# A gated feed-forward kernel: the first weights of block 3 issued later than those of block 2

## The chip, the cores and the metric

The kernel runs on one core of one Trainium2 chip. The metric is the device time of one execution in microseconds (us). A profile covers a slightly shorter span, from the program's first instruction to its last (297.6 us for a run timed at 299.36 us).

## The reference

```python
B, S, D, F = 32, 32, 1024, 3584        # x: (B, S, D), weights scaled by 0.05, all bf16
def reference(x, w_gate, w_up, w_down):
    return (_gelu(x @ w_gate) * (x @ w_up)) @ w_down
```

There are 1024 rows of x. The contraction over D is done in 8 blocks of 128, called block 0 to block 7 below.

## The kernel before

A small program builder records operations in order and derives semaphore waits from what each reads (`r`) and writes (`w`). All operations are emitted from a helper, so most lines of the profile carry the helper's line number (L98). They are told apart by tile names: `wg` and `wu` are the gate and up weights, `xT` the transposed x, `xn` the untransposed first part of x, `ps` the accumulators.

From 0.77 us the matrix engine runs 8 matmuls on constants, called warm-up matmuls below. The real work should start at once, but x must first be transposed and the weights must first arrive. Blocks 0 and 1 of x come as plain loads and are transposed on the matrix engine. Blocks 2 to 7 come by transposing loads on the sync queue. The first group of weights comes in pieces, on the sync and the scalar queue.

```python
NX = 2
for i, eng in enumerate(("sp", "act")):                     # x of blocks 0 and 1, untransposed
    pr.add(eng, "dma_start", xn[...], x_r[...], w=[("xn", i)], dma=f"xn{i}")
for k in range(NX):
    load_w("sp", "g", 0, k, k + 1)                          # gate weights of block k, 128 KB
    load_w("act", "u", 0, k, k + 1)                         # up weights of block k, 128 KB
...
for k0, k1 in ((2, 3), (3, 4), (4, 5), (5, 6), (6, 8)):
    load_x(0, k0, k1)                                       # transposing loads, sync queue
load_w("act", "g", 0, 2, 4)                                 # weights of blocks 2 and 3: 256 KB
load_w("act", "u", 0, 2, 4)                                 #   and another 256 KB
pr.add("act", "activation", warm[:, 0:1], const0, ACTF.Gelu_apprx_tanh)
for k in range(NX):                                         # transpose blocks 0 and 1, copy to xT
    ...
    pr.add("dve", "tensor_copy", xT[:, k, i * 256:(i + 1) * 256], half, r=[("ps", b)],
           w=[("x", k, 0) if i == 0 else ("x", k, "b")])
# ... [cut] then, for the first 512 rows: blocks 0 to 5, each 4 gate and 4 up matmuls;
# after the last matmul of block 0 the scalar queue issues the weights of blocks 4 and 5,
# after the last one of block 1 those of blocks 6 and 7:
if k < 2:
    load_w("act", "g", 0, 2 * k + 4, 2 * k + 6, r=[("mm", k)])
    load_w("act", "u", 0, 2 * k + 4, 2 * k + 6)
```

## Time and profile before

| What | Value |
|---|---|
| time, first 3 runs | 300.06 us median (299.14 to 300.2) |
| span of the profiled run | 297.6 us |
| matrix engine busy | 294.3 us |
| start-to-start time of two matmuls, 512 columns | 0.216 us |
| hole before the matmuls of block 2 | 0.35 us |
| hole after that, to the end | none |

The page of the kernel before starts with the busy time of each engine and the granted clock of the matrix engine (its clock as a share of full speed, in tenths) in 40 slices. It also names the chain of work that ended last.

```profile
span 297.6 us, 2575 instructions
PE 294.3 (99%) x1388; PEld 78.2 (26%) x808; DVE 42.7 (14%) x68; ACT 37.3 (13%) x67; POOL 0.7 (0%) x6
PEclk9999999999999999999999999999999999999999
PE 96%; DMA 2%; SPq 0%; issue 0%; ACT 0%
PE ps L98 54%; PE ps L163 42%; DMA xT<-in_x_dram 2%; SPq L98 0%; ACT xT L98 0%
```

The matrix engine is the bound. Only 2% of the chain is something else: a transposing load of x. The chain in order of time, for the first 12 us (start, duration, what), shows which one:

```profile
2.21 6.22 DMA xT<-in_x_dram
8.43 0.14 issue
8.56 3.61 PE ps L98 x16
```

The load of x block 2 was issued at 2.21 us and landed at 8.43 us. The matmuls of block 2 start at 8.56 us. What that costs is read from the timeline of the matrix engine from 7 to 9.2 us, whose first and last group are cut by that window (start, busy time, group, and in brackets the idle time before it):

```profile
6.70 0.81 PE L98 MATMUL ps<-xT,wg 128*128 128x512 bf16 x3
7.35 1.03 PE L98 MATMUL ps<-xT,wu 128*128 128x512 bf16 x4
8.56 0.81 PE L98 MATMUL ps<-xT,wg 128*128 128x512 bf16 x3 [0.19 <-DMA xT<-in_x_dram]
```

The idle time in brackets counts from the modelled end of the last matmul, and matmuls overlap. So the cost is read from the starts. Four matmuls take 4 x 0.216 = 0.863 us, and block 2 could have started at 7.35 + 0.863 = 8.21 us. It started 0.35 us later. Below, "hole" always means this: a start-to-start time minus 0.216 us.

### The profile page before, as it was taken

How to read it: one execution, taken by the hardware profiler on the slowest of the kernel's cores; microseconds unless marked ns; L12 is line 12 of the kernel's file. 1: busy time of each engine (PE TensorE's matmuls, PEld its weight loads, DVE VectorE, ACT ScalarE, POOL GpSimd, SP SyncE). 2: the span in 40 equal slices, each digit the busy share in tenths (PEclk: the TensorE clock that was granted, in tenths of full speed). 3: DMA queues.
4: the chain of work that ended last, by engine and by line, in shares of the span. 5: the costliest groups of instructions: out<-in, count | busy, mean ns of one | idle time of the engine just before them, and what ended most of it. 6: DMA issues, size and time to landing. Idle time of an engine off the chain costs nothing.

```text
span 297.6 us, 2575 instructions
## 1 busy us (share of the span) xinstructions
PE 294.3 (99%) x1388; PEld 78.2 (26%) x808; DVE 42.7 (14%) x68; ACT 37.3 (13%) x67; POOL 0.7 (0%) x6
## 2 busy tenths in 40 slices
PE   8999999999999999999999999999999999999997
PEld 4444322222222222222222222222222222222244
DVE  1030311111221111111111122110000000000000
ACT  1030411111111111221111111110000000000010
POOL 0000000000000000000000000000000000000000
PEclk9999999999999999999999999999999999999999
DMA  7999743006708409321030040000101101011011
GB/s 207 252 241 353 226 134 134 9 0 189 234 2 270 154 2 330 94 76 65 0 139 4 0 141 0 0 2 0 35 0 35 37 0 35 0 37 35 0 35 35
DMA packets 28842, 26.37 MB, mean 89 GB/s; under 512 B 8352, under 2 KB 25248, under 8 KB 28832
## 3 DMA queue, kind: packets, MB, share of 16 engines
q1 hardware_dynamic: 26640, 24.25, 26.3%
q10 hardware_dynamic: 2192, 1.97, 2.2%
q8 instruction: 8, 0.13, 0.2%
q14 instruction: 2, 0.02, 0.0%
HBM read 22.28 MB, written 2.10 MB: 82 GB/s over the span
## 4 chain that ended last, share of the span: by engine, by line
PE 96%; DMA 2%; SPq 0%; issue 0%; ACT 0%
PE ps L98 54%; PE ps L163 42%; DMA xT<-in_x_dram 2%; SPq L98 0%; ACT xT L98 0%
## 5 line engine op out<-in xcount | busy, mean ns | idle before, releaser
L98 PE MATMUL ps<-xT,wg 128*128 128x512 bf16 x256 | 90.2, 379 | 0.4 <-DVE xT L98 0.2
L98 PE MATMUL ps<-xT,wu 128*128 128x512 bf16 x256 | 90.2, 379 | 0.0
L98 PE MATMUL ps<-wd,hT 128*128 128x512 bf16 (+2 forms) x280 | 86.6, 358 | 0.0
L163 PE MATMUL ps<-wd,hT 128*128 128x512 bf16 x196 | 74.3, 379 | 0.0
L163 PE MATMUL ps<-xT,wg 128*128 128x512 bf16 x192 | 72.8, 379 | 0.0
L163 PE MATMUL ps<-xT,wu 128*128 128x512 bf16 x192 | 72.8, 379 | 0.0
L98 DVE TENSOR_TENSOR hT<-g,ps 128x512 bf16<-128x512 f32 x56 | 36.4, 685 | 158.5 <-PE ps L98 158.5
L98 ACT ACTIVATE g<-ps 128x512 f32<-128x512 f32 x56 | 30.8, 595 | 160.4 <-PE ps L98 160.4
L98 PEld LDWEIGHTS ps<-wd,hT 128*128 128x128 bf16 x280 | 26.0, 98 | 71.3 <-issue 65.8
L98 PEld LDWEIGHTS ps<-xT,wu 128*128 128x128 bf16 x256 | 25.0, 98 | 71.7 <-issue 64.1
L98 PEld LDWEIGHTS ps<-xT,wg 128*128 128x128 bf16 x256 | 24.9, 98 | 72.0 <-issue 64.8
L98 DVE CAST xT<-ps 128x512 bf16<-128x512 f32 (+1 forms) x8 | 5.4, 680 | 89.6 <-ACT xT L98 79.8
L98 ACT ACTIVATE xT<-ps 128x512 bf16<-128x512 f32 (+1 forms) x9 | 5.0, 558 | 94.6 <-PE ps L98 94.6
L98 PE MATMUL ps<-const-bfloat16-1.0 128*128 128x1024 fp8e4 (+1 forms) x8 | 3.0, 558 | 0.8 <-PEq L310 0.8
L98 PEld LDWEIGHTS ps<-const-bfloat16-1.0 128*128 128x256 fp8e4 x8 | 1.7, 218 | 1.9 <-issue 1.9
L98 ACT ACT_TABLE_LOAD x1 | 1.3, 1283 | 3.4 <-issue 3.4
L98 DVE COPY xT<-ps 128x256 bf16<-128x256 bf16 x4 | 0.9, 286 | 4.1 <-PE ps L98 4.1
L98 PE MATMUL ps<-ident,xn 128*128 128x128 bf16 x8 | 0.9, 278 | 0.0
L98 PEld LDWEIGHTS ps<-ident,xn 128*128 128x128 bf16 x8 | 0.6, 124 | 0.2
L98 POOL TENSOR_SCALAR_AFFINE_SELECT ident<-ident 128x128 bf16<-128x128 bf16 x1 | 0.3, 292 | 0.2 <-POOL ident L98 0.2
L98 POOL MEMSET ident<- 128x128 bf16 x1 | 0.2, 204 | 0.3 <-POOLq L310 0.3
L98 ACT ACTIVATE warm<-const-float32-0.0 128x1 f32<-128x1 f32 x1 | 0.2, 202 | 0.0
(4 smaller groups left out, 0.4 us busy)
## 6 DMA issues: line engine op xcount, KB each, us to landing
wd<-in_w_down_dram SPq DMA_DIRECT2D x7, 1024.0 KB, 5.4
wg<-in_w_gate_dram SPq DMA_DIRECT2D x6, 1024.0 KB, 7.4
wu<-in_w_up_dram SPq DMA_DIRECT2D x6, 1024.0 KB, 9.7
out_dram<-xT SPq DMA_DIRECT2D x15, 128.0 KB, 1.7
wg<-in_w_gate_dram ACTq DMA_DIRECT2D x3, 256.0 KB, 4.5
wu<-in_w_up_dram ACTq DMA_DIRECT2D x3, 256.0 KB, 4.9
wg<-in_w_gate_dram SPq DMA_DIRECT2D x2, 128.0 KB, 3.2
wu<-in_w_up_dram ACTq DMA_DIRECT2D x2, 128.0 KB, 3.5
```

Source lines behind the costliest of these rows:

```text
L98: ins = name(eng, *args, **kw) if callable(name) else getattr(eng, name)(*args, **kw)
L163: return eng.add_instruction(mybir.InstMatmult(start_tensor_calc=start, stop_tensor_calc=stop, ldweights=False, name=nc.get_next_instructi ...
```

## The change

The intent is to let x of block 2 land sooner. Its packets share the DMA engines with 512 KB of weights, half of which (block 3) is not needed for another 1.7 us. The change splits those weights and holds back the half for block 3 until the copy of x block 1.

```diff
-        load_w("act", "g", 0, 2, 4)
-        load_w("act", "u", 0, 2, 4)
+        load_w("act", "g", 0, 2, 3)
+        load_w("act", "u", 0, 2, 3)
         pr.add("act", "activation", warm[:, 0:1], const0, ACTF.Gelu_apprx_tanh)
         for k in range(NX):
             ...
+        load_w("act", "g", 0, 3, 4, r=[("x", 1, 0)])
+        load_w("act", "u", 0, 3, 4)
```

## The prediction

> **What bounds the kernel.** The matrix engine. In the profile page it is busy 294.3 of 297.6 us; the chain of waits is 96% matmuls and 2% one DMA, the transposing load of x. In the timeline one matmul starts per 0.216 us (863 ns for four) from 8.56 us to the end, granted clock 1.00. Nothing after 8.56 us waits for data. Ahead of that are two holes: 0.2 us at 4.76 us (the copy of x block 0, untouched by the change) and one at block 2. Four matmuls of block 1 start at 7.35, so block 2 could start at 8.21; it starts at 8.56, just after the transposing load of x block 2 landed at 8.43 (6.2 us after its issue at 2.21; the other transposes of the first half took 4.7 to 5.3, those of the second half, with quieter queues, 3.5 to 3.7). So the whole prize is about 0.35 us, 0.12%.
>
> **What the change does.** Before, the scalar queue issues 256 KB of gate weights (2.27 us, landed 6.72) and 256 KB of up weights (2.75, landed 8.28) for blocks 2 and 3. After, only the halves for block 2 go then; 256 KB for block 3 wait for the third vector copy (copies run 4.07 to 5.01), so until about 4.8 us. Two more DMA issues (about 0.45 us each) run on the scalar queue from 4.8 to 5.8, before its next issue at 6.68, which waits for the matrix engine anyway.
>
> The Trainium skill, "DMA: Bandwidth & Descriptors", sections "Queues, rings and completion order" and "Issuing engines are not separate DMA queues", says both queues share the same 16 engines, taking turns by packet. The trace agrees: in the packet records the 256-byte packets of x block 2 (about 32 an engine, 18 to 24 ns each) spread over 4.6 to 7.0 us while some 33 weight packets of 1 KB an engine (46 to 73 ns) stand in the other queue. With 16 of them gone I estimate 16 x 55 ns = 0.9 us off the load of x block 2: landing at 7.0 to 7.6 instead of 8.43. That removes the wait at block 2, and no more.
>
> **What it may cost.** Block 3 would be needed at 9.94 (gate) and 10.8 (up). Issued at 4.85 and 5.3, and taking 4 to 4.9 us as the other weights of that time, they land near 9.0 and 9.8: slack about 1 us, thin, since they now meet the transposes of blocks 3 and 4. A miss would give back 0.2 to 1 us.
>
> **Predicted.** Most likely the wait vanishes: 300.06 - 0.35 = 299.7 us, less than the run spread of 1.06 us. Range 298.9 to 300.6. Faster by over 2%: 0.01; within 2%: 0.98; slower by over 2%: 0.01.
>
> **What would show it.** Timeline: block 2 starts near 8.2 and no start-to-start step above 0.25 us afterwards; the chain of waits no longer holds the transposing load of x; span near 297.2. DMA issue list: gate and up weights in pieces of 128 KB, block 3 issued near 4.85. The last 280 us are unchanged.
>
> **What would make it wrong.** The landing of x block 2 does not hang on the weights (its completion records came late, amid a stretch of stalled packets at 7.2 to 8.2 us, in which only 157 GB/s moved): then block 2 stays at 8.5. Or the later weights queue behind the transposes' descriptors (the gate weights issued at 6.68 had no packet before 9.0) and block 3 waits: a new hole near 10 us, 0.2 to 1 us slower.

## The result, and the profile after

A ratio here is the mean time of one kernel's fast runs over that of the other's fast runs of the same rounds, so it is not quite the ratio of the medians. Executions over 1.5% slower than the fastest of the same kernel are left out of the means.

The first measurement gave 300.26 us median (6 runs, 299.37 to 1792.36) beside 300.13 us for the kernel before (6 runs). The ratio was 1.0001, with a 95% interval of 0.9976 to 1.0025. No difference.

One run took 1792 us, and the profile happened to fall on it. Nearly every matmul in it was slow while the vector and scalar engines were not. The first lines and three groups of its page (after the bar: busy us, mean ns of one, idle before):

```profile
span 1790.6 us, 2579 instructions
PE 1787.7 (100%) x1388; PEld 260.1 (15%) x808; DVE 45.1 (3%) x68; ACT 39.9 (2%) x67; POOL 0.7 (0%) x6
L98 PE MATMUL ps<-xT,wu 128*128 128x512 bf16 x256 | 420.9, 1709 | 0.0
L98 DVE TENSOR_TENSOR hT<-g,ps 128x512 bf16<-128x512 f32 x56 | 38.5, 688 | 1146.0 <-PE ps L98 1131.4
L98 ACT ACTIVATE g<-ps 128x512 f32<-128x512 f32 x56 | 33.4, 597 | 1137.6 <-PE ps L98 1120.0
```

A matmul took 1709 ns instead of 379 ns, while the vector and scalar operations kept their usual length (688 against 685 ns, 597 against 595 ns). Two matmuls started 1.278 us apart (median) instead of 0.216 us. That looks like a lower clock of the matrix engine, but the profile holds no clock record, so it is not shown. It did not come back in the other 23 runs of this kernel, so it explains nothing about the change and is left out of every comparison. A fast profile of the changed kernel had to be taken anew, and the first experiments below give three.

The page of the first of these (changed kernel, 298.92 us), to be set beside the lines of before:

```profile
span 297.1 us, 2579 instructions
PE 294.0 (99%) x1388; PEld 78.3 (26%) x808; DVE 42.6 (14%) x68; ACT 37.3 (13%) x67; POOL 0.7 (0%) x6
```

Its chain in order of time, first 14 us, and then its timeline around block 2:

```profile
0.77 3.26 PE ps L98 x10
4.03 0.02 issue
4.06 0.50 DVE xT L98 x2
4.56 0.14 issue
4.69 9.44 PE ps L98 x43
```

```profile
7.28 1.03 PE L98 MATMUL ps<-xT,wu 128*128 128x512 bf16 x4
8.14 1.03 PE L98 MATMUL ps<-xT,wg 128*128 128x512 bf16 x4
9.01 0.38 PE L98 MATMUL ps<-xT,wu 128*128 128x512 bf16 x1
```

The load of x has left the chain. Block 2 starts at 8.14 us, exactly 0.86 us after the group before it, and this run has no hole at all from its first real matmul to its end. Its span, 297.1 us, therefore serves below as the span without a hole. In this profile the change did what the prediction said. The times do not show it, and that is what the experiments are about.

### The profile page after: what moved, and what is told of

It reads as the page before. It is cut to its first block, busy times and chain, and to the rows that moved or that the text cites. A ratio compares the mean times of both kernels' runs of the same rounds, so it can differ in the third digit from the quotient of the medians.

```text
span 1790.6 us, 2579 instructions
## 1 busy us (share of the span) xinstructions
PE 1787.7 (100%) x1388; PEld 260.1 (15%) x808; DVE 45.1 (3%) x68; ACT 39.9 (2%) x67; POOL 0.7 (0%) x6
## 4 chain that ended last, share of the span: by engine, by line
PE 100%; ACT 0%; issue 0%
PE ps L98 57%; PE ps L163 43%; ACT xT L98 0%
## 5 line engine op out<-in xcount | busy, mean ns | idle before, releaser
L98 PE MATMUL ps<-xT,wu 128*128 128x512 bf16 x256 | 420.9, 1709 | 0.0
L98 PE MATMUL ps<-xT,wg 128*128 128x512 bf16 x256 | 420.2, 1704 | 0.0
L98 PE MATMUL ps<-wd,hT 128*128 128x512 bf16 (+2 forms) x280 | 408.7, 1572 | 0.0
L163 PE MATMUL ps<-wd,hT 128*128 128x512 bf16 x196 | 334.5, 1707 | 0.0
L163 PE MATMUL ps<-xT,wg 128*128 128x512 bf16 x192 | 327.9, 1708 | 0.0
L163 PE MATMUL ps<-xT,wu 128*128 128x512 bf16 x192 | 327.3, 1705 | 0.0
L98 PEld LDWEIGHTS ps<-wd,hT 128*128 128x128 bf16 x280 | 89.0, 323 | 506.6 <-issue 506.6
L98 PEld LDWEIGHTS ps<-xT,wu 128*128 128x128 bf16 x256 | 83.2, 325 | 509.5 <-issue 508.5
L98 PEld LDWEIGHTS ps<-xT,wg 128*128 128x128 bf16 x256 | 82.1, 321 | 506.0 <-issue 504.9
L98 PE MATMUL ps<-const-bfloat16-1.0 128*128 128x1024 fp8e4 (+1 forms) x8 | 8.8, 1466 | 0.8 <-PEq L313 0.8
```

The source lines that it names most:

```text
L98: ins = name(eng, *args, **kw) if callable(name) else getattr(eng, name)(*args, **kw)
L163: return eng.add_instruction(mybir.InstMatmult(start_tensor_calc=start, stop_tensor_calc=stop, ldweights=False, name=nc.get_next_instructi ...
```

## The experiments

### The same two kernels again, and each half of the change

`before_again` and `after_again` are the two kernels unchanged. The other two take the change apart:

```diff
 # pieces_only, against the kernel before
-        load_w("act", "g", 0, 2, 4)
-        load_w("act", "u", 0, 2, 4)
+        for k in (2, 3):
+            load_w("act", "g", 0, k, k + 1)
+            load_w("act", "u", 0, k, k + 1)
 # defer_both, against the changed kernel
-        load_w("act", "g", 0, 2, 3)
-        load_w("act", "u", 0, 2, 3)
 ...
-        load_w("act", "g", 0, 3, 4, r=[("x", 1, 0)])
+        load_w("act", "g", 0, 2, 3, r=[("x", 1, 0)])
+        load_w("act", "u", 0, 2, 3)
+        load_w("act", "g", 0, 3, 4)
         load_w("act", "u", 0, 3, 4)
```

> The kernel before, unchanged, once more, timed against itself: how far one profile can be trusted for a few tenths of a us. Both theories: ratio 1.000, interval about 0.25% either way. The transposing load of x block 2 lands at 8.4 us, give or take 0.3 if landings vary from run to run; block 2 of the matmuls starts right behind it, if that is later than 8.21.

Measured: ratio 0.9989 (0.9972 to 1.0006), so two copies of one kernel can look 0.1% apart. x landed at 8.95 us, later than the 8.1 to 8.7 us expected. The profile has two holes: 0.66 us at block 2 behind that load, and 0.26 us at block 1, whose gate weights landed at 6.65 us.

> The changed kernel, unchanged, because its only profile fell in a run of 1790 us. Theory A (weight packets in the other queue hold up the load of x block 2): it lands at 7.0 to 7.7 us, block 2 starts at 8.2 with no hole, span 0.3 us shorter than that of the kernel before. Theory B (the load is held up by its own path: descriptors, transposing writes, stalls of the engines, whatever the weights do): it lands at 8.0 to 8.5, block 2 starts within 0.15 us of where it did. Either way the weights of block 3 land by 9.9 and 10.8 us with no new hole; if one is there near 10 us, it ate the gain. Ratio 0.999 to 1.001.

Measured: ratio 1.0001 (0.9976 to 1.0026). x of block 2 landed at 7.34 us, as theory A said; no hole. The weights of block 3 were issued at 4.77 and 5.15 us and landed at 8.59 and 9.72 us, in time for 9.87 and 10.73 us.

> The split into pieces without the wait: gate 2, up 2, gate 3, up 3 issued one behind the other from 2.27 us. Same bytes in the same stretch as before. Theory A: x block 2 lands as in the kernel before (8.2 to 8.5), hole of about 0.35 us stays. Theory B: the same, so this run only says whether the split alone does something. Ratio 1.000.

Measured: ratio 0.9994 (0.9978 to 1.0011). x of block 2 landed at 8.74 us, hole 0.59 us. In this one profile the split alone did not bring the load forward.

> The weights of block 2 wait for the copy of x block 1 as well, so that no weight packet of blocks 2 or 3 is there before about 6 us. Theory A: x block 2 lands clearly earlier than in the changed kernel, at 6.0 to 7.0 us. Theory B: still at 7.8 or later. The matmuls of block 2 now wait for their weights instead (issued near 4.85, 4 to 4.5 us to land: about 9 us), so a new hole of 0.5 to 1.5 us before block 2; ratio 1.001 to 1.005.

Measured: 301.56 us, ratio 1.0048 (1.0031 to 1.0066). x of block 2 landed at 6.40 us. The weights of block 2 landed at 8.30 and 9.31 us, earlier than expected, and cost only 0.17 us. The loss came elsewhere. The up weights of blocks 4 and 5, which are issued behind the pushed-back pieces, took 7.5 us to land. From the chain in order of time of `defer_both`:

```profile
7.41 7.48 DMA wu<-in_w_up_dram
14.89 0.05 issue
14.94 2.12 PE ps L98 x9
```

That wait is a hole of 2.05 us.

How long the transposing load of x block 2 takes, from issue to landing, is one line per profile. In order: `before`, `before_again`, `pieces_only`, `after_again`, `defer_both`. The first two carry the bytes of blocks 2 and 3 beside the load in two big pieces, `pieces_only` in four, the changed kernel carries half of them, and the last none.

```profile
DMA to landing us min/median/max: 6.2/6.2/6.2
```
```profile
DMA to landing us min/median/max: 6.7/6.7/6.7
```
```profile
DMA to landing us min/median/max: 6.5/6.5/6.5
```
```profile
DMA to landing us min/median/max: 5.1/5.1/5.1
```
```profile
DMA to landing us min/median/max: 4.2/4.2/4.2
```

These five order as theory A says: the fewer weight packets beside it, the sooner the load lands. In the kernel before, 490 of the load's 512 packets had started by 7.0 us; in `after_again`, 499 packets of 256 bytes by 6.0 us. That speaks against theory B, by which the weights do not matter. But it is a tendency, and the next section has profiles that break it. Over all profiles whose sync queue is unchanged, the load took 4.8 to 6.7 us with all those bytes beside it (five profiles, mean 6.0), and 4.8 to 5.8 us with half of them (six, mean 5.3). In the same profiles the last of the 512 packets started at 6.43 to 7.47 us (mean 7.0) and at 5.99 to 6.76 us (mean 6.4), and the load landed another 0.6 to 1.5 us later. So part of the spread lies after the packets, where nothing here explains it.

### More samples, and the load of x issued sooner

`after_b`, `after_c` and `before_b` are again the unchanged kernels. `x2_sooner` moves one weight piece from the sync to the scalar queue:

```diff
 # x2_sooner, against the changed kernel
-            load_w("sp", "g", 0, k, k + 1)
+            load_w("act" if k else "sp", "g", 0, k, k + 1)
```

> The changed kernel again, for a second and third sample of where its holes lie. The spans say that every run's holes can be read without a profile: 297.1 us is the span without a hole (first profile of this kernel), and the five other runs beside it had 297.4 to 299.7. Theory H1 (the wait at block 2 is gone in nearly every run, and the later weights, of blocks 3 to 5, have become late instead in most): a profile of 297.8 us or more shows holes at 9.9 us or later, waiting for weights. Theory H2 (the load of x block 2 still comes too late in most runs, 8.2 us or more, and the first profile was a lucky one): the hole stands at block 2 again. Ratio 0.998 to 1.001 either way.

Measured: ratio 1.0008 (0.9985 to 1.0032), five fast runs with spans of 297.4 to 299.5 us, and one slow (304.35 us, mean granted clock 0.994; not profiled, so its cause is open). The profile: no hole at block 2 (x landed at 7.49 us), but one of 0.13 us at block 4, at 11.87 us, whose gate weights landed at 11.83 us. The profile's span fell under the 297.8 us for which the expectation was written. What it shows has H1's form, but is small.

> The same kernel once more; as after_b. If H1 holds, holes of two profiles with spans over 297.5 both lie at blocks 3 to 5; if H2, at block 2.

Measured: ratio 0.9989 (0.9974 to 1.0004). No hole at all, x landed at 7.48 us. Three fast profiles of the changed kernel, three times no hole at block 2: that speaks against H2. It does not rule it out, because the profiles happened to fall on fast runs: the fastest of this kernel's six in `after_again` and in `after_b`, the second fastest here, none with a span over 297.5 us. H1, a loss at later weights "in most" runs, is not borne out either: one of three, and 0.13 us. The slower runs, for which both were written, were not seen.

> The kernel before, third sample of its holes. Both theories: first and largest hole at block 2 (about 8.5 to 9.1 us), behind the load of x block 2, sum of holes 0.3 to 1.2 us; ratio 1.000.

Measured: ratio 0.9992 (0.9979 to 1.0004). The expectation failed. There is no hole at block 2 here: x landed at 7.01 us, in the unchanged kernel and with all the weights beside it. That is sooner than in the two profiles of the changed kernel of the same call. How long the load took, in order `before_b`, `after_b`, `after_c`:

```profile
DMA to landing us min/median/max: 4.8/4.8/4.8
```
```profile
DMA to landing us min/median/max: 5.3/5.3/5.3
```
```profile
DMA to landing us min/median/max: 5.3/5.3/5.3
```

So the order of the first call is reversed in the second, and theory A is not shown for single runs. The run of `before_b` lost 0.42 us all the same, in the first three matmuls. The view by form for 4.6 to 7 us shows it (after the bar: busy us, mean ns of one, idle before); first `before_b`, then `after_again`:

```profile
L98 PE MATMUL ps<-xT,wg 128*128 128x512 bf16 x5 | 1.8, 479 | 0.0
L98 PE MATMUL ps<-xT,wu 128*128 128x512 bf16 x4 | 1.0, 379 | 0.0
```
```profile
L98 PE MATMUL ps<-xT,wg 128*128 128x512 bf16 x7 | 1.8, 378 | 0.3 <-DVE xT L98 0.3
L98 PE MATMUL ps<-xT,wu 128*128 128x512 bf16 x4 | 1.0, 379 | 0.0
```

A full-speed matmul has 376 to 379 ns here, so a mean of 479 ns means that some ran slower: the first of them started 381 and 427 ns apart instead of 216 ns. The matrix engine was still at half clock. The Trainium skill, "TensorE: Matmul & The Clock Gate", section "What's actually happening", says that the array starts at half clock, that a busy window of about 3.4 us raises it, and that the window runs freely, so that the moment varies by run. The traces agree on the steps, 427 ns first and 216 ns later. The clock record has the rise at 4.27 us in the kernel before, 4.04, 5.00 and 4.39 us in the three profiles of the changed one, 5.61 us in `before_b` and 6.25 us in `x2_sooner`. Real matmuls begin at 4.7 us, so a late rise costs up to 0.97 us in the profiles, leaving `late_start` aside (`before_w5_dropped` below; it has no clock record, like `before_again` and `defer_both`, and its loss is read from the steps).

> On top of the change, the gate weights of block 1 are issued from the scalar queue, so that the transposing load of x block 2 is issued 0.45 us sooner (1.74 instead of 2.21) and up 1, gate 2 and up 2 0.45 us later. H2: the load lands about 0.4 us sooner than in the changed kernel in the same call, hole at block 2 smaller, mean time 0.2 to 0.4 us shorter. H1: the mean time stays or grows, because the weights (block 1 needed at 6.5, block 2 at 8.2) now come later; holes at up weights of block 1 or gate weights of block 2.

Measured: 300.59 us, ratio 1.0024 (1.0010 to 1.0039), so a small loss. The load of x was issued at 1.75 us and landed at 8.56 us, after 6.8 us instead of 5.1 to 5.3. In this profile, issuing it sooner did not make it land sooner. That the time grew is what H1 said, but not where: the large hole is at the weights of blocks 4 and 5, as the chain in order of time shows:

```profile
7.38 6.17 DMA wg<-in_w_gate_dram
13.55 0.04 issue
13.59 1.47 PE ps L98 x6
```

That is a hole of 1.02 us; another 0.74 us of its 1.95 us went to the late clock and 0.20 us to two small holes.

### Is it the clock, the weights of blocks 4 and 5, or chance?

```diff
 # late_start, against the changed kernel; the real matmuls also wait for "go"
+        for i in range(12):
+            pr.add("dve", "memset", g_b[0][:, :], 0.0, r=["go"], w=["go"])
+        for n in [512] * 14:
+            pr.add("pe", "matmul", ps[:, 3, 0:n], ...)      # more warm-up matmuls
 # w45_sooner, against the changed kernel
         load_w("act", "u", 0, 3, 4)
+        load_w("act", "g", 0, 4, 6)
+        load_w("act", "u", 0, 4, 6)
 ...
-                    if k < 2:
+                    if k == 1:
 # w5_dropped, against the changed kernel; before_w5_dropped, against the kernel before.
 # Wrong on purpose: block 5 of the first group uses block 4's weights.
+            kw = 4 if m < 4 and k == 5 else k               # and kw for k in the weight operand
-                        load_w("act", "g", 0, 2 * k + 4, 2 * k + 6, r=[("mm", k)])
-                        load_w("act", "u", 0, 2 * k + 4, 2 * k + 6)
+                        k1 = 2 * k + (6 if k else 5)
+                        load_w("act", "g", 0, 2 * k + 4, k1, r=[("mm", k)])
+                        load_w("act", "u", 0, 2 * k + 4, k1)
```

> On top of the change: twelve memsets chained on the vector engine hold the first real matmul back to about 9 to 11 us, and fourteen more warm-up matmuls keep the matrix engine busy meanwhile, so that its clock has risen and x and the weights of blocks 0 to 3 have landed before the real work starts. It is slower on purpose. Theory V (all of the run-to-run spread of both kernels is made in the first 12 us, by late data and by the matmuls that still run at half speed, 427 ns a step instead of 216, until 4.3 to 6.5 us): its runs agree within 0.3 us. Rival (spread made later, in the long weight-bound stretch or at the end, so that it has nothing to do with the change): its runs spread over 1 us or more as those of the other kernels do.

Measured: 308.98 us, spans 306.7 to 308.9 us. The experiment failed as built. Each memset took 0.66 us with its wait, so the real work started at 12.93 us, when the extra warm-up matmuls had long ended. The engine idled 4.8 us and its clock fell again. Three stretches of its view by windows (stretch, its length, busy us of the engines with instruction counts, granted clock, DMA share, GB/s):

```profile
4.00:9.00 5.00, 4.16 (x21) 2.51 (x18) 3.86 (x10) 0.93 (x2) 0.00 (x0) 1.00 1.21 212
13.00:16.00 3.00, 3.00 (x9) 1.03 (x10) 0.00 (x0) 0.00 (x0) 0.00 (x0) 0.56 0.00 0
16.00:21.00 5.00, 5.00 (x25) 2.29 (x24) 0.00 (x0) 0.00 (x0) 0.00 (x0) 1.00 0.57 177
```

The clock was granted at 0.56 on average between 13 and 16 us, and only 9 matmuls started there. So the start was no steadier than before, and theory V was not tested. It did show 1.32 us lost to half-speed matmuls after the idle time.

> On top of the change: the weights of blocks 4 and 5 are issued straight behind those of block 3 (about 5.8 us) instead of waiting for the last matmul of block 0 (6.6 us), so ahead of the transposing load of x block 5 in the queues. Theory H1 (the rest of what the change should have gained is lost at blocks 4 and 5, whose weights landed 0.0 to 0.6 us before or after they were needed in the profiles): they land 0.5 us or more sooner, no span over 298.7, mean time 0.2 to 0.4 us under that of the kernel before. Rival (the loss lies with the clock's rise or in chance): nothing changes beyond 0.1 us, ratio 0.999 to 1.001.

Measured: ratio 1.0003 (0.9980 to 1.0026), spans 297.5 to 299.5 us. The weights of blocks 4 and 5 were issued at 5.72 and 6.21 us, 0.9 us sooner than in `after_again`, but landed at 11.47 and 12.82 us, later than there (10.97 and 11.75 us). The up weights made a hole of 0.29 us. H1's expectation failed. The chain in order of time:

```profile
6.21 6.62 DMA wu<-in_w_up_dram
12.82 0.05 issue
12.87 2.33 PE ps L98 x10
```

What was issued sooner here took longer to land. This version is not measurably faster than either kernel.

> Wrong on purpose: on top of the change, the weights of block 5 of the first group are not loaded (256 KB less in the crowded stretch) and its matmuls use those of block 4. H1: the weights of block 4 land about 1 us sooner, no hole after 9 us, spans 297.1 to 298.2, ratio about 0.998. Rival: ratio 0.999 to 1.001 with spans to 299 and above still there.

Measured: wrong result; ratio 0.9984 (0.9963 to 1.0005), spans 297.2 to 298.2 us, one hole of 0.04 us at block 2, where x landed at 8.06 us. Spans and ratio are H1's, but not the way there: the weights of block 4 landed at 11.01 and 11.48 us, not about 1 us sooner than those of blocks 4 and 5 in `after_again` (10.97 and 11.75 us). And the interval includes 1, so it proves little without its control.

> Wrong on purpose, the control to the run before it: the same 256 KB of block 5 are left out, but without the change. Its spans were 297.2 to 298.2 with the change. Theory H1 (without the change the loss is made at block 2, where block 5's bytes are not yet in the way; the change moves it to blocks 4 and 5): nothing is gained, hole at block 2 still there, spans 297.5 to 299.0 as those of the kernel before, ratio 0.9995 to 1.0005. Rival (256 KB less in the first 12 us helps either kernel alike, and the change does nothing): spans 297.2 to 298.2, ratio about 0.998.

Measured: ratio 0.9986 (0.9963 to 1.0009), spans 297.1 to 298.2 us. This is what the rival said: leaving those bytes out comes out alike with and without the change, so H1 gets no support from the pair. Nor is the rival proved, since both intervals include 1. The two were timed in different calls, too. Its profile repeats `before_b`: no hole at block 2, because x landed at 7.77 us, before 8.16 us, when block 2 could have started at full clock; and 0.97 us lost to half-speed matmuls. The form view for 4.6 to 7 us:

```profile
L98 PE MATMUL ps<-xT,wg 128*128 128x512 bf16 x4 | 1.9, 620 | 0.1
L98 PE MATMUL ps<-xT,wu 128*128 128x512 bf16 x3 | 1.0, 437 | 0.0
```

### The fast profiles together

Those of `defer_both`, `x2_sooner` and `late_start` are described above and left out here. All in us; the losses are start-to-start times above 0.216 us, summed.

| Profile | Span | x block 2 landed | Lost at block 2 | Lost to half clock | Lost elsewhere |
|---|---|---|---|---|---|
| before | 297.56 | 8.43 | 0.35 | 0 | 0 |
| before_again | 298.08 | 8.95 | 0.66 | 0 | 0.26, block 1 |
| before_b | 297.60 | 7.01 | 0 | 0.42 | 0 |
| pieces_only | 297.86 | 8.74 | 0.59 | 0.13 | 0 |
| before_w5_dropped | 298.12 | 7.77 | 0 | 0.97 | 0 |
| after_again | 297.14 | 7.34 | 0 | 0 | 0 |
| after_b | 297.42 | 7.49 | 0 | 0.13 | 0.13, block 4 |
| after_c | 297.23 | 7.48 | 0 | 0 | 0 |
| w45_sooner | 297.55 | 6.95 | 0 | 0.06 | 0.29, block 4 |
| w5_dropped | 297.18 | 8.06 | 0.04 | 0 | 0 |

(The remaining differences of span, up to 0.1 us, are the start of the first real matmul, 4.69 to 4.80 us.)

All fast runs of the two unchanged kernels together: 22 of the changed kernel average 299.87 us (298.92 to 301.49), 61 of the kernel before 299.86 us (298.93 to 301.17). Resampling these runs puts the difference of the means between -0.30 and +0.34 us, 19 times in 20. So a gain of 0.35 us lies just outside what the times allow. The spans say the same: the 22 average 298.07 us, and the 55 of the kernel before that the record lists 298.04 us. Against 297.14 us without a hole, both kernels lose about 0.9 us in a mean run. And two of those 55 had 297.1 and 297.2 us, so the kernel before can also run with next to no hole.

## Why the prediction was right or wrong

The predicted 299.7 us (298.9 to 300.6), within 2%, held: 300.26 us in the first measurement, 299.7 us as the median of the 22 fast runs. That says nothing for the mechanism. The 61 fast runs of the kernel before have a median of 299.75 us, so the range would have held for a change that does nothing, and the agreement with 299.7 us is luck: the gain it was to come from is not in the times.

- **"Most likely the wait vanishes", block 2 starts near 8.2 us.** Right in the profiles: none of the three fast ones of the changed kernel has the hole, and the load has left the chain. But `before_b` has no hole there either, without the change.
- **"I estimate 16 x 55 ns = 0.9 us off the load ... landing at 7.0 to 7.6."** Right for the landing: 7.34, 7.49 and 7.48 us (6.95, 7.76 and 8.06 us in the three variants with the same loads up to block 3). In the mean of all such profiles the gain is about 0.7 us, in the packets and in the landing, but the two groups overlap. The mechanism, two queues that take turns on the same engines, is that of the Trainium skill, "DMA: Bandwidth & Descriptors", sections "Queues, rings and completion order" and "Issuing engines are not separate DMA queues". The series 6.2, 6.7 and 6.5, then 5.1, then 4.2 us supports it; `before_b`, with 4.8 us against 5.3 us twice, does not. That packets take turns one by one is not shown: the records kept do not name the DMA engine of a packet.
- **"Block 3 ... near 9.0 and 9.8".** Right: 8.59 and 9.72 us in `after_again`, 8.72 and 10.11 us in `after_b`, 9.20 and 10.12 us in `after_c`, all before they were needed.
- **"So the whole prize is about 0.35 us", "300.06 - 0.35".** This is the step that was too simple. It took one profile for the kernel. Over three profiles of the kernel before, the hole was 0.35, 0.66 and 0 us. The 0 came because the load landed at 7.01 us, 1.2 us before block 2 could have started at full clock (8.18 us). The late clock of that run is not the reason. The load took 4.8 to 6.7 us in one and the same kernel, a spread far larger than the prize. Where the load is late and the clock too, the losses overlap instead: in `x2_sooner` x landed at 8.56 us, 0.4 us after block 2 could have started (8.16 us), but the slow matmuls had moved that start to 8.91 us, and no hole shows. And the average of the times shows no gain.
- **"No start-to-start step above 0.25 us afterwards".** Wrong once in three: 0.35 us before block 4 in `after_b`. The prediction looked for the next late piece at block 3; the next one was the weights of blocks 4 and 5, which were needed sooner now but landed no sooner. The x of block 4 even landed later: at 8.64 to 10.64 us in the five profiles with the weights of blocks 2 and 3 up front (mean 9.8), at 9.96 to 10.96 us in the six with those of block 3 pushed back (mean 10.5). `defer_both` (2.05 us), `x2_sooner` (1.02 us) and `w45_sooner` (0.29 us) waited at the same blocks. That the slower runs of the changed kernel lose time there too is only an inference: they were not profiled.

What stays open: the three fast profiles of the changed kernel have spans of 297.1 to 297.4 us, but its 22 fast runs average 298.1 us. The runs with spans of 299.0 to 299.7 us were not profiled, so where they lost 1.9 to 2.6 us is unknown. The test that should have told whether all spread arises in the first 12 us (`late_start`) failed, and the pair with block 5 left out did not separate the theories. It is equally open how much of the missing 0.35 us is a loss given back at blocks 4 and 5, how much was no gain to begin with, because the load is often early enough in the kernel before, and how much is chance.

## What to carry to other kernels

Holding back transfers that are not needed yet brought forward the one that was waited for, here by 0.7 us in the mean and not in every run, but it moves the same bytes: the piece pushed back is the next candidate to be late, so list for every later piece when it lands and when it is needed. Where the possible gain is smaller than the run-to-run spread, take several profiles of both kernels before naming a hole, and compare holes rather than times. And check whether a wait runs beside a second loss, here the half clock of the first microseconds, because removing one of two overlapping losses can gain nothing, as the hidden wait of `x2_sooner` shows.

## What the Trainium skill lacked or had wrong

- "TensorE: Matmul & The Clock Gate", section "What you observe", has the clock's rise vary by 500 ns either way. Here the clock record has it at 4.04 to 6.25 us, with the same first matmul at 0.77 us: a range of 2.2 us, and 0 to 0.97 us lost in the profiles.
- The same page, section "Seeing it yourself", warns that the clock events are unreliable and that the clock has been seen stuck at a quarter for 50 us and more. Here the matmuls were slower and for longer: 1.278 us from start to start instead of 0.216 us, nearly a sixth of the rate, through a run of 1790.6 us. That this is the clock is likely but not shown: the profile holds no clock record, as three ordinary ones here do not either, and the run's listed mean clock is 1.0.
- No page says how to read the time before the first clock record. The views used here count it as 1.00: in `before_b` they do so from 4.7 to 5.6 us, while real matmuls start 427 ns apart. The step between matmuls is the safer witness.
- "DMA: Bandwidth & Descriptors" gives no figure for how much the latency of a transposing load beside other traffic varies from run to run. Here one and the same load, in one and the same kernel, took 4.8, 6.2 and 6.7 us from issue to landing.
